# Two transformer layers on one core: column blocks of 512 + 64 in place of 288 + 288 in the MLP output and the projections

## The chip, the cores and the metric

The kernel runs on one core of a Trainium2 chip. The metric is the device time of one execution in microseconds (us), the median of several executions. TensorE, ScalarE, VectorE, GpSimdE and SyncE are called PE, ACT, DVE, POOL and SP, as in the profile. PEld is PE's weight load. L776 is line 776 of the kernel's file; the two files have different line numbers.

## The reference

```python
# B=1, S=2048 tokens, D=576, H=32 heads of 18, window 256, F=4608
def A(x, wqkv, wo):                       # sliding-window causal attention
    q, k, v = split(x @ wqkv)             # (2048 x 576) @ (576 x 1728)
    s = q @ k.T * 18**-0.5                # masked: 0 <= i - j < 256
    return softmax(s) @ v @ wo            # @ (576 x 576)
def Bm(x, w1, b1, w2, b2):
    return gelu(layernorm(x) @ w1 + b1) @ w2 + b2    # 576 -> 4608 -> 576
x = A_x
for _ in range(2):
    x = x + A(layernorm(x), A_wqkv, A_wo)
    x = x + Bm(layernorm(x), B_w1, B_b1, B_w2, B_b2)
```

## The kernel before

The work is cut into 8 chunks: two layers with four chunks of four 128-token tiles each. For every chunk there are projections (`qkv`), attention (`E`, in two halves of four head groups), the attention output (`tail`) and an MLP in two halves of F (`G_part`, `mm2`). Different chunks overlap. While the attention of chunk k runs, PE also does the MLP output of earlier chunks and the projections of the next one. I call this the filling work, because it fills the time in which ACT computes exponentials.

Nothing is ordered at run time. When the kernel is built, its own planner assigns each task a start from assumed costs and emits one fixed order for each engine. It also picks a PSUM bank for each task.

```python
FILL = (6, 5, 4)        # banks for the filling work: projections, attention output, MLP output
MM1 = (0, 1, 2, 3)      # first MLP matmul
SC = (0, 2, 4)          # pairs of banks (0,1), (2,3), (4,5) for the scores; a score group takes two pairs
...
def mm_cost(n):         # assumed time of one matmul of n columns, us
    return max(n / 2400.0, 0.026) + (0.006 if n > 64 else 0.0)
...
def place(t):           # planner: which bank
    ...
    key = (max(bank_free[b] for b in bs), n)     # the bank that has been free longest, then list order
```

Each output row has 576 columns, more than the 512 fp32 columns that the program counts as one PSUM bank (`bank(i)` is `ps[:, i*512:(i+1)*512]`), so every product is cut in columns. Before, the cut is 288 + 288.

```python
def mm2(k, hf, prio):                     # MLP output of one half of F (18 blocks of 128)
    for i in range(nt):                   # four token tiles
        for hh in range(2):               # two halves of 288 columns
            b = Bank(FILL)
            for f0 in range(0, NFH, 6):   # one PE task: 6 matmuls
                ... e.matmul(bank(b)[:, 0:HB], hT[:, fl, tile i], w2_sb[:, fl, hh*HB:(hh+1)*HB],
                             start=(fl == 0), stop=(fl == NFH - 1))
            resid(t, hh, b, prio)         # DVE adds the bank to x: the bank is free after that
def two_out(...):                         # projections and attention output: two banks of 288
    for o in range(2): 5 matmuls of 288 columns (576 = 4.5 x 128 rows, padded with zeros)
# qkv: two_out for q, for k, for v; a DVE cast for each bank
def scores(k, g, parts, prio):            # 32-row matmuls, four at a time; then two exponentials on ACT
    bs = [Bank(SC, True), Bank(SC, True)]
```

The softmax here doesn't subtract the row's maximum and nothing guards it: scores larger than these inputs give would overflow.

## Time and profile before

| what | before |
|---|---|
| median of 6 runs | 985.98 us (983.5 to 988.68) |
| span of the profiled run | 987.9 us |
| PE busy | 949.5 us (96%) |
| next engine: ACT busy | 586.0 us (59%) |

The profiled execution took 989.72 us, a little more than the slowest of the six.

The first lines are from the page of the kernel before: span, busy time with share and number of instructions, and the chain that ended last as shares of the span.

```profile
span 987.9 us, 22924 instructions
PE 949.5 (96%) x9592; PEld 606.9 (61%) x9592; DVE 317.1 (32%) x772; ACT 586.0 (59%) x705; POOL 368.8 (37%) x507
PE 78%; DMA 5%; DVE 5%; POOL 5%; ACT 4%; issue 3%; DVEq 0%; POOLq 0%
```

PE bounds the kernel. The next lines are groups of instructions of the same page: line, engine, operation, tiles, shapes and count, then busy time and the mean of one in ns, then idle time just before them and what ended it.

```profile
L637 ACT ACTIVATE pT<-ps 128x1024 bf16<-128x1024 f32 (+2 forms) x384 | 347.2, 971 | 128.1 <-PE ps L628 126.9
L776 PE MATMUL ps<-w_sb,hT 128*128 128x288 bf16 x2304 | 316.1, 288 | 6.0 <-DVE x_res L709 4.9
L709 DVE TENSOR_TENSOR x_res<-ps,x_res 128x288 f32<-128x288 f32 x160 | 70.7, 449 | 363.4 <-PE ps L776 342.6
L558 PE MATMUL ps<-wqkv,xnTa 128*128 128x288 bf16 x768 | 120.5, 286 | 8.9 <-DVE qn L594 5.0
L509 DVE TENSOR_SCALAR xn<-x_res,mv_all,rstd 128x576 bf16<-128x576 f32 x60 | 47.2, 801 | 26.1 <-POOL rstd L499 14.6
```

The mean of 288 ns is not what a matmul costs in a stream, because the records of successive matmuls overlap. The start times in the trace show that cost. From one L776 matmul to the next the median is 122 ns, from one L751 matmul (512 columns) to the next it is 216 ns, against a mean record of 379 ns.

The first of these lines reads: ACT stood idle for 126.9 us in front of exponentials because it waited for score matmuls (L628).

The waits view says who waited for whom: total us, times, longest.

```profile
PE ps L628 <- ACT pT L637: 8.4, 18, 1.4
PE ps L558 <- DVE qn L594: 5.0, 5, 1.0
PE ps L776 <- DVE x_res L709: 4.9, 10, 0.6
```

### The profile page before, as it was taken

To read this page: it belongs to the slowest core of one execution; us is meant where nothing else is said; L and a number is where in the kernel's file an instruction comes from. 1 tells how busy PE (TensorE), PEld (TensorE's weight loads), DVE (VectorE), ACT (ScalarE), POOL (GpSimd) and SP (SyncE) were. 2 spreads that over 40 slices of the span, in tenths; PEclk is the share of its full clock that TensorE was granted. 3 is DMA by queue.
4 is the path that set the end of the run, shared out by engine and by line. 5 is a ranking of instruction groups with operands and counts; after the bars stand their busy time and mean duration, and the time that the engine had idled before them with its cause. 6 is when DMAs were issued, how large, how long until landed. Compare 5 with 4: busy or idle time off the path is not lost.

```text
span 987.9 us, 22924 instructions
## 1 busy us (share of the span) xinstructions
PE 949.5 (96%) x9592; PEld 606.9 (61%) x9592; DVE 317.1 (32%) x772; ACT 586.0 (59%) x705; POOL 368.8 (37%) x507
## 2 busy tenths in 40 slices
PE   8898889999999999999999999999999999999998
PEld 6665547655575656756476565756567564657556
DVE  5653612722145211534028130361115310132001
ACT  0476676377753777447761777627774487852531
POOL 4555725334333434325153252433333352531000
PEclk9999899999999999999999999999999999999999
DMA  9846380964269250881529542494516816084540
GB/s 195 173 116 136 74 253 15 208 174 138 68 145 192 60 178 28 188 187 34 191 56 204 136 126 80 133 170 106 169 49 167 177 44 198 14 220 118 172 132 25
DMA packets 227287, 129.58 MB, mean 131 GB/s; under 512 B 141808, under 2 KB 225008, under 8 KB 227184
## 3 DMA queue, kind: packets, MB, share of 16 engines
q1 hardware_dynamic: 217872, 120.43, 49.4%
q0 software_dynamic: 6880, 5.03, 2.7%
q10 hardware_dynamic: 2432, 2.65, 0.9%
q8 instruction: 76, 1.25, 0.5%
q14 instruction: 27, 0.22, 0.1%
HBM read 90.69 MB, written 2.36 MB: 94 GB/s over the span
## 4 chain that ended last, share of the span: by engine, by line
PE 78%; DMA 5%; DVE 5%; POOL 5%; ACT 4%; issue 3%; DVEq 0%; POOLq 0%
PE ps L776 29%; PE ps L751 27%; PE ps L558 7%; PE ps L675 7%; PE ps L628 6%; ACT pT L637 3%; POOL pT L658 2%; DMA attT<-attq 2%; DVE x_res L709 2%; PE ps L564 2%; POOL rstd L499 2%; DVE st_all L486 2%; DMA x_res<-in_A_x_dram 1%; DMA kT<-qn 1%; DVE xn L509 1%
## 5 line engine op out<-in xcount | busy, mean ns | idle before, releaser
L637 ACT ACTIVATE pT<-ps 128x1024 bf16<-128x1024 f32 (+2 forms) x384 | 347.2, 971 | 128.1 <-PE ps L628 126.9
L658 POOL TENSOR_SCALAR_AFFINE_SELECT pT<-pT 128x512 bf16<-128x512 bf16 (+1 forms) x368 | 278.1, 778 | 388.2 <-ACT pT L637 365.4
L755 ACT ACTIVATE hT<-ps,b1col 128x512 bf16<-128x512 f32 x288 | 196.5, 687 | 251.1 <-PE ps L751 250.8
L776 PE MATMUL ps<-w_sb,hT 128*128 128x288 bf16 x2304 | 316.1, 288 | 6.0 <-DVE x_res L709 4.9
L751 PE MATMUL ps<-xnTm,w_sb 128*128 128x512 bf16 x1440 | 319.4, 379 | 0.1
L776 PEld LDWEIGHTS ps<-w_sb,hT 128*128 128x128 bf16 x2304 | 211.2, 98 | 80.6 <-issue 20.2
L751 PEld LDWEIGHTS ps<-xnTm,w_sb 128*128 128x128 bf16 x1440 | 139.5, 98 | 159.6 <-issue 0.4
L709 DVE TENSOR_TENSOR x_res<-ps,x_res 128x288 f32<-128x288 f32 x160 | 70.7, 449 | 363.4 <-PE ps L776 342.6
L558 PE MATMUL ps<-wqkv,xnTa 128*128 128x288 bf16 x768 | 120.5, 286 | 8.9 <-DVE qn L594 5.0
L675 PEld LDWEIGHTS ps<-vA,pT 128*128 128x128 bf16 x2880 | 94.2, 96 | 29.2 <-issue 11.7
L675 PE MATMUL ps<-vA,pT 128*128 128x20 bf16 x2880 | 100.6, 172 | 5.6 <-DVE attq L690 2.7
L558 PEld LDWEIGHTS ps<-wqkv,xnTa 128*128 128x128 bf16 x768 | 71.2, 97 | 33.1 <-DVE qn L594 7.8
L628 PE MATMUL ps<-qT,kT 32*128 32x384 bf16 (+2 forms) x1408 | 75.0, 280 | 11.6 <-ACT pT L637 8.4
L594 DVE CAST qn<-ps 128x288 bf16<-128x288 f32 x128 | 57.4, 455 | 39.2 <-PE ps L564 38.3
L486 DVE BATCH_NORM_STATS2 st_all<-x_res 128x6 f32<-128x288 f32 x120 | 50.8, 446 | 17.2 <-DMA x_res<-in_A_x_dram 15.9
L509 DVE TENSOR_SCALAR xn<-x_res,mv_all,rstd 128x576 bf16<-128x576 f32 x60 | 47.2, 801 | 26.1 <-POOL rstd L499 14.6
L564 PE MATMUL ps<-wqkv,xnTa 128*128 128x288 bf16 x192 | 54.9, 286 | 0.0
L628 PEld LDWEIGHTS ps<-qT,kT 32*128 32x128 bf16 x1408 | 22.4, 92 | 49.0 <-issue 24.7
L733 POOL TENSOR_TENSOR x_res<-x_res,b2bc 128x576 f32<-128x576 f32 x32 | 45.2, 1415 | 13.7 <-DVE xn L509 12.9
L712 DVE TENSOR_TENSOR xn<-ps,x_res 128x288 bf16<-128x288 f32 x32 | 14.6, 458 | 110.9 <-PE ps L776 110.9
L497 POOL TENSOR_SCALAR vtmp<-mv_all 128x1 f32<-128x1 f32 (+1 forms) x43 | 8.6, 200 | 103.9 <-DVE mv_all L488 101.4
L685 DVE RECIPROCAL rinv<-ps 128x16 f32<-128x16 f32 x64 | 16.4, 257 | 95.7 <-PE ps L675 95.4
(32 smaller groups left out, 332.7 us busy)
## 6 DMA issues: line engine op xcount, KB each, us to landing
w_sb<-in_B_w_dram SPq DMA_DIRECT2D x144, 288.0 KB, 5.1
w_sb<-in_B_w_dram SPq DMA_DIRECT2D x72, 512.0 KB, 4.0
w_sb<-in_B_w_dram SPq DMA_DIRECT2D x72, 64.0 KB, 3.7
x_res<-in_A_x_dram POOLq DMA_DIRECT2D x4, 1152.0 KB, 7.0
out_dram<-xn SPq DMA_DIRECT2D x16, 144.0 KB, 1.8
wqkv<-in_A_wqkv_dram ACTq DMA_DIRECT2D x3, 576.0 KB, 5.9
hT<-in_A_x_dram SPq DMA_DIRECT2D x1, 576.0 KB, 5.2
wo_sb<-in_A_wo_dram ACTq DMA_DIRECT2D x1, 576.0 KB, 4.0
```

The costliest lines, as they stand in the source:

```text
L486: add("dve", lambda e, i=i, s=s: e.bn_stats(st_all[:, t, i, :], s[:, t, i * HB:(i + 1) * HB]), reads=res, writes=[f"st{t}_{i}"], cost=0.43 ...
L558: ins = e.matmul(bank(bs[o])[:, 0:n], lhs(o, c, full), rhs(o, c, full), start=(c == 0), stop=False)
L564: ins = e.matmul(bank(bs[o])[:, 0:n], lhs(o, 4, full), rhs(o, 4, full), start=False, stop=True)
L594: add("dve", lambda e, o=o, b=bs[o], qv=qv: e.tensor_copy(qv[:, o * 16:(o + 1) * 16, 0:DH], bank(b)[:, 0:HB].rearrange("p (h d) -> p h d", ...
L628: ins = e.matmul(two(bs[j // 2])[:, j % 2, col:col + nq * 128], kT[32 * j:32 * j + 32, g, (T0 + so) % KS, :], qT[32 * j:32 * j + 32, g, qo ...
L637: add("act", lambda e, h2=h2: e.activation(pT[:, sl, 2 * h2:2 * h2 + 2, lo:hi], two(bs[h2])[:, :, lo:hi], ACT.Exp, scale=SCALE), reads=[bs ...
L658: add("pool", lambda e, ap=ap, pat=pat, sgn=sgn, kind=kind: e.affine_select(ap, ap, pattern=pat, compare_op=(ALU.is_ge if kind == "d" else ...
L675: ins = e.matmul(bank(B_O)[:, o:o + VW], pT[:, sl, j, col + qi * 128:col + (qi + 1) * 128], vA[:, (T0 + so) % VS, 4 * g + j, :], start=(fi ...
L709: add("dve", lambda e: e.tensor_tensor(x_res[:, t, sl], bank(b)[:, 0:HB], x_res[:, t, sl], ALU.add), reads=[b], writes=[f"x{t}h{hh}"], cos ...
L751: ins = e.matmul(bank(bk)[:, 0:n], w1_sb[:, sl, col:col + 128], xnTm[:, k % 2, c, 0:n], start=(c == 0), stop=(c == KD - 1))
L755: add("act", lambda e, f=f, fl=fl, bk=bk: e.activation(hT[:, fl, 0:n], bank(bk)[:, 0:n], ACT.Gelu_apprx_tanh, bias=b1col[:, f:f + 1]), rea ...
L776: ins = e.matmul(bank(b)[:, 0:HB], hT[:, fl, i * 128:(i + 1) * 128], w2_sb[:, fl, hh * HB:(hh + 1) * HB], start=(fl == 0), stop=(fl == NFH ...
```

## The change

The cut becomes 512 + 64 (504 + 72 in the projections, where heads of 18 must stay whole). Its intent is to have fewer and longer groups of matmuls, with the short blocks collected in one bank: those of four token tiles in the MLP output, those of q, k and v in the projections. One assumed cost of the planner changes too, from 6 to 4 ns per matmul. The removed `PAIR` branches were dead code.

```diff
-        return max(n / 2400.0, 0.026) + (0.006 if n > 64 else 0.0)
+        return max(n / 2400.0, 0.026) + (0.004 if n > 64 else 0.0)
 # qkv
-            bs = two_out(...)                       # 2 banks x 5 matmuls of 288, for q, k and v each
+        main(0); main(1)                            # 5 matmuls of 504 columns each, a bank each
+        rest((0, 1, 2))                             # 15 matmuls of 72 columns, one bank, start only on the first
+        transpose(0); transpose(1)
+        main(2)
 # tail: 5 x (512 columns, 64 columns) into two banks
 # mm2
-        for i in range(nt):
-            for hh in range(2):                     # 18 matmuls of 288, then resid
+        b = Bank(FILL)
+        for f0 in range(0, NFH, 6):                 # short blocks of four tiles first, one bank
+            for fl in range(f0, f0 + 6):
+                for i in range(nt):
+                    ... e.matmul(bank(b)[:, i*64:(i+1)*64], hT[:, fl, tile i], w2_sb[:, fl, 512:D],
+                                 start=(fl == 0 and i == 0), ...)
+        ... one addition for the four short blocks
+        for i in range(nt):
+            b = Bank(FILL)
+            for f0 in range(0, NFH, 6):             # one PE task: 6 matmuls of 512
+                ... e.matmul(bank(b), hT[:, fl, tile i], w2_sb[:, fl, 0:512], ...)
+            resid(t, 0, b, ...)
 # cuts: resid, ln_stats and pv follow the new columns and heads; PAIR branches removed
```

Four accumulations share one bank here, and only the first matmul carries the start flag. The Trainium skill, "PSUM — Partial Sum Buffer", "The four PSUM rules", names this form as one of two that work: a start clears the written marks of the whole bank, and the other groups' first matmuls find them clear and overwrite.

More of the change, by code (lines that the diff above doesn't have):

```diff
@@ L331, in schedule @@
         return max(t.end for t in self.tasks)
-PAIR = False
-W1W = 2560
 WARM_UNTIL = 140.0
@@ L352, in build_kernel @@
     HB = 288
+    DS = (slice(0, 512), slice(512, 576))
     VW = 20
@@ L373, in build_kernel @@
     x_res = sb("x_res", [P, NT, D], FP32)
-    w1_sb = sb("w1_sb", [P, NB1, W1W], BF16)
+    w1_sb = sb("w1_sb", [P, NB1, 2560], BF16)
     w2_sb = sb("w2_sb", [P, NFH, D], BF16)
@@ L449, in build_kernel @@
     add("pool", lambda e: e.memset(nhalf[:, :], -0.5), writes=["nhalf"], cost=0.1, prio=-10)
-    if not PAIR:
-        add("pool", lambda e: e.memset(xn[:, :, D:KD * 128], 0.0), writes=[f"xn{i}" for i in range(NXN)], cost=0.4, prio=-10)
+    add("pool", lambda e: e.memset(xn[:, :, D:KD * 128], 0.0), writes=[f"xn{i}" for i in range(NXN)], cost=0.4, prio=-10)
     add("pool", lambda e: e.memset(vA[:, :, :, DH:VW], 1.0), writes=[f"v{s}h{h}" for s in range(VS) for h in range(2)], cost=1.6, prio=-8)
@@ L455, in build_kernel @@
             writes=[f"qn{i}h{h}" for h in range(2)], cost=0.5, prio=-9)
-    if not PAIR:
-        add("pool", lambda e: e.memset(attq[:, :, D:KD * 128], 0.0), writes=["aqd"], cost=0.5, prio=-8)
-        add("dve", lambda e: e.memset(wqkv[64:128, 4, :], 0.0), writes=["wqC", "wkC", "wvC"], cost=1.0, prio=-8)
-        add("dve", lambda e: e.memset(wo_sb[64:128, 4, :], 0.0), writes=["woC"], cost=0.4, prio=-8)
-        add("dve", lambda e: e.memset(w1_sb[64:128, :, 2048:2560], 0.0), writes=["w1Z"], cost=1.0, prio=-8)
+    add("pool", lambda e: e.memset(attq[:, :, D:KD * 128], 0.0), writes=["aqd"], cost=0.5, prio=-8)
+    add("dve", lambda e: e.memset(wqkv[64:128, 4, :], 0.0), writes=["wqC", "wkC", "wvC"], cost=1.0, prio=-8)
+    add("dve", lambda e: e.memset(wo_sb[64:128, 4, :], 0.0), writes=["woC"], cost=0.4, prio=-8)
+    add("dve", lambda e: e.memset(w1_sb[64:128, :, 2048:2560], 0.0), writes=["w1Z"], cost=1.0, prio=-8)
     dma("pool", b2bc[:, :], bass.AP(tensor=B_b2.tensor, offset=B_b2.offset, ap=[[0, P], [1, D]]), writes=["b2"], cls="b", ring=2,
@@ L483, in ln_stats @@
         for i in range(2):
-            res = [f"x{t}h{i}"] if srcres is None else [srcres]
+            res = X(t)[:i + 1] if srcres is None else [srcres]
             s = x_res if src is None else src
@@ L512, in ln_norm_T @@
         rd = [f"xn{sl}"]
-        if PAIR:
-            add("dve", lambda e: e.tensor_scalar(xn[:, sl, D:KD * 128], s[:, t, 512:D], mv_all[:, t, 0:1], rstd[:, t:t + 1],
-                                                  op0=ALU.subtract, op1=ALU.mult),
-                reads=res + [f"mv{t}", f"rstd{t}"], writes=[f"xd{sl}"], cost=0.12, prio=prio)
-            rd.append(f"xd{sl}")
         add("sp", lambda e: e.dma_start_transpose(dst[:, :, i * 128:(i + 1) * 128], xn[:, sl, :]),
@@ L533, in w1_load @@
             reads=reads, writes=[f"w1a{sl}"], cls="w1", cost=0.5, prio=prio)
-        if PAIR:
-            src = B_w1[512:576, cols].rearrange("p (a b f) -> p b a f", a=2, b=2)
-            for b in range(2):
-                dma("sp", w1_sb[64 * b:64 * b + 64, sl, 2048:2304].rearrange("p (a f) -> p a f", a=2), src[:, b],
-                    writes=[f"w1b{sl}_{b}"], cls="w1", cost=0.5, prio=prio)
-        else:
-            dma("sp", w1_sb[0:64, sl, 2048:2560], B_w1[512:576, cols], reads=["w1Z"], writes=[f"w1b{sl}_0"], cls="w1", cost=0.5,
-                prio=prio)
+        dma("sp", w1_sb[0:64, sl, 2048:2560], B_w1[512:576, cols], reads=["w1Z"], writes=[f"w1b{sl}_0"], cls="w1", cost=0.5, prio=prio)
     def w2_load(hf, prio, gate=False):
@@ L547, in w2_load @@
                 reads=[f"h{2 * pr}"] if gate else [], writes=[f"w2s{pr}"], cls="w2", ring=9, cost=0.6, prio=prio)
-    def two_out(lhs, rhs, n, reads, prio, after=()):
-        bs = [Bank(FILL), Bank(FILL)]
-        full = slice(0, 128)
-        for o in range(2):
-            def fn(e, o=o):
-                ins = None
-                for c in range(4):
-                    ins = e.matmul(bank(bs[o])[:, 0:n], lhs(o, c, full), rhs(o, c, full), start=(c == 0), stop=False)
-                if PAIR and o == 1:
-                    for oo in range(2):
-                        r = slice(64 * oo, 64 * oo + 64)
-                        ins = e.matmul(bank(bs[oo])[:, 0:n], lhs(oo, 4, r), rhs(oo, 4, r), start=False, stop=True, tile_position=(64 * oo, 0))
-                if not PAIR:
-                    ins = e.matmul(bank(bs[o])[:, 0:n], lhs(o, 4, full), rhs(o, 4, full), start=False, stop=True)
-                return ins
-            w = [bs[0], bs[1]] if (o == 1 and PAIR) else [bs[o]]
-            cost = mm_cost(n) * (4 if PAIR else 5) + (mm_cost(n) * 1.2 if PAIR and o == 1 else 0.0)
-            add("pe", fn, reads=reads, writes=w, cost=cost, prio=prio, alloc=((bs if o == 0 else ()) if PAIR else [bs[o]]), after=after)
-        return bs
     qn_ctr = [0]
-    qn_at = {}
     def qkv(k, i, prio):
@@ L577, in qkv @@
         A = l * NT + t0 + i
-        for n, w in enumerate("qkv"):
-            dest = [f"v{A % VS}h{o}" for o in range(2)] if w == "v" else [f"qn{qn_ctr[0] % NQN}h{o}" for o in range(2)]
-            bs = two_out(lambda o, c, r: xnTa[r, c, i * 128:(i + 1) * 128],
-                         lambda o, c, r, n=n: wqkv[r, c, n * D + o * HB:n * D + (o + 1) * HB], HB,
-                         [f"w{w}A", f"w{w}B", f"w{w}C", f"xa{i}"], prio + 0.01 * n, after=dest)
-            if w == "v":
-                sv = A % VS
-                for o in range(2):
-                    add("dve", lambda e, o=o, b=bs[o]: e.tensor_copy(vA[:, sv, o * 16:(o + 1) * 16, 0:DH],
-                                                                   bank(b)[:, 0:HB].rearrange("p (h d) -> p h d", d=DH)),
-                        reads=[bs[o]], writes=[f"v{sv}h{o}"], cost=0.42, prio=prio)
-            else:
-                sl = qn_ctr[0] % NQN
-                qn_ctr[0] += 1
-                qv = qn[:, sl, :].rearrange("p (h e) -> p h e", e=32)
-                for o in range(2):
-                    add("dve", lambda e, o=o, b=bs[o], qv=qv: e.tensor_copy(qv[:, o * 16:(o + 1) * 16, 0:DH],
-                                                                          bank(b)[:, 0:HB].rearrange("p (h d) -> p h d", d=DH)),
-                        reads=[bs[o]], writes=[f"qn{sl}h{o}"], cost=0.42, prio=prio)
-                if w == "q":
-                    dst, dn = qT[:, :, i * 128:(i + 1) * 128], f"q{i}"
-                else:
-                    dst, dn = kT[:, :, A % KS, :], f"k{A % KS}"
-                add("sp", lambda e, dst=dst, sl=sl: e.dma_start_transpose(dst, qn[:, sl, :]),
-                    reads=[f"qn{sl}h0", f"qn{sl}h1"], writes=[dn], dma="t", ring=8, cost=1.3, lat=2.5, move=0.6, prio=prio)
@@ new lines, in qkv, with main, fn @@
+        sv = A % VS
+        sls = [(qn_ctr[0] + n) % NQN for n in range(2)]
+        qn_ctr[0] += 2
+        views = [qn[:, sl, :].rearrange("p (h e) -> p h e", e=32) for sl in sls] + [vA[:, sv, :, :]]
+        names = [[f"qn{sl}h{o}" for o in range(2)] for sl in sls] + [[f"v{sv}h{o}" for o in range(2)]]
+        wr = lambda n: [f"w{'qkv'[n]}{x}" for x in "ABC"]
+        def main(n):
+            b = Bank(FILL)
+            def fn(e):
+                ins = None
+                for c in range(KD):
+                    ins = e.matmul(bank(b)[:, 0:504], xnTa[:, c, i * 128:(i + 1) * 128], wqkv[:, c, n * D:n * D + 504], start=(c == 0),
+                                   stop=(c == KD - 1))
+                return ins
+            add("pe", fn, reads=wr(n) + [f"xa{i}"], writes=[b], cost=mm_cost(504) * KD, prio=prio + 0.01 * n, alloc=[b], after=names[n][:1])
+            add("dve", lambda e: e.tensor_copy(views[n][:, 0:28, 0:DH], bank(b)[:, 0:504].rearrange("p (h d) -> p h d", d=DH)),
+                reads=[b], writes=names[n][:1], cost=0.68, prio=prio)
@@ new lines, in rest, with fn @@
+        def rest(ns):
+            b = Bank(FILL)
+            def fn(e):
+                ins = None
+                for c in range(KD):
+                    for n in ns:
+                        ins = e.matmul(bank(b)[:, n * 72:(n + 1) * 72], xnTa[:, c, i * 128:(i + 1) * 128],
+                                       wqkv[:, c, n * D + 504:(n + 1) * D], start=(c == 0 and n == ns[0]),
+                                       stop=(c == KD - 1 and n == ns[-1]), skip_group_check=True)
+                return ins
+            add("pe", fn, reads=[r for n in ns for r in wr(n)] + [f"xa{i}"], writes=[b], cost=0.033 * len(ns) * KD, prio=prio, alloc=[b],
+                after=[names[n][1] for n in ns])
+            for n in ns:
+                add("dve", lambda e, n=n: e.tensor_copy(views[n][:, 28:32, 0:DH], bank(b)[:, n * 72:(n + 1) * 72].rearrange("p (h d) -> p h d", d=DH)),
+                    reads=[b], writes=names[n][1:], cost=0.2, prio=prio)
@@ new lines, in transpose @@
+        def transpose(n):
+            if n == 0:
+                dst, dn = qT[:, :, i * 128:(i + 1) * 128], f"q{i}"
+            else:
+                dst, dn = kT[:, :, A % KS, :], f"k{A % KS}"
+            add("sp", lambda e: e.dma_start_transpose(dst, qn[:, sls[n], :]), reads=names[n], writes=[dn], dma="t", ring=8, cost=1.3,
+                lat=2.5, move=0.6, prio=prio)
+        main(0)
+        main(1)
+        rest((0, 1, 2))
+        transpose(0)
+        transpose(1)
+        main(2)
@@ L679, in fn @@
             return ins
-        rd = [f"p{sl}h0", f"p{sl}h1"] + [f"p{sl}m{i}" for i in range(3)] + [f"v{(T0 + p[0]) % VS}h{g // 4}" for p in parts]
+        rd = [f"p{sl}h0", f"p{sl}h1"] + [f"p{sl}m{i}" for i in range(3)] + [f"v{(T0 + p[0]) % VS}h{g // 7}" for p in parts]
         add("pe", fn, reads=rd, writes=[f"pb{B_O}"], cost=0.026 * 4 * sum(p[2] for p in parts), prio=prio, lat=0.2)
@@ L703, in E, with resid @@
             pv(k, *p, prio - 0.1)
-    def resid(t, hh, b, prio, outp=None):
-        src = bank
-        sl = slice(hh * HB, (hh + 1) * HB)
+    def resid(t, hh, b, prio, outp=None, col=0):
+        sl = DS[hh]
+        n = sl.stop - sl.start
         if outp is None:
-            add("dve", lambda e: e.tensor_tensor(x_res[:, t, sl], bank(b)[:, 0:HB], x_res[:, t, sl], ALU.add),
-                reads=[b], writes=[f"x{t}h{hh}"], cost=0.46, prio=prio)
-        else:
-            add("dve", lambda e: e.tensor_tensor(xn[:, outp, sl], bank(b)[:, 0:HB], x_res[:, t, sl], ALU.add),
-                reads=[b, f"x{t}h{hh}"], writes=[f"xn{outp}" if hh == 0 else f"xd{outp}"], cost=0.46, prio=prio)
+            add("dve", lambda e: e.tensor_tensor(x_res[:, t, sl], bank(b)[:, col:col + n], x_res[:, t, sl], ALU.add),
+                reads=[b], writes=[f"x{t}h{hh}"], cost=(0.74, 0.2)[hh], prio=prio)
+        else:
+            add("dve", lambda e: e.tensor_tensor(xn[:, outp, sl], bank(b)[:, col:col + n], x_res[:, t, sl], ALU.add),
+                reads=[b, f"x{t}h{hh}"], writes=[f"xn{outp}"], cost=(0.74, 0.2)[hh], prio=prio)
     def tail(k, prio):
@@ L717, in tail @@
         rd = [f"aq{g}" for g in range(G)]
-        if PAIR:
-            add("dve", lambda e: e.tensor_copy(attq[:, 0:nt, D:KD * 128], attq[:, 0:nt, 512:D]), reads=rd, writes=["aqd"], cost=0.25,
-                prio=prio)
         for i in range(nt):
@@ L725, in tail, with fn @@
             t = t0 + i
-            bs = two_out(lambda o, c, r, i=i: attT[r, c, i * 128:(i + 1) * 128],
-                         lambda o, c, r: wo_sb[r, c, o * HB:(o + 1) * HB], HB, [f"aT{i}", "woA", "woB", "woC"], prio)
+            bs = [Bank(FILL), Bank(FILL)]
+            def fn(e, i=i, bs=bs):
+                ins = None
+                for c in range(KD):
+                    for o in range(2):
+                        ins = e.matmul(bank(bs[o])[:, 0:(512, 64)[o]], attT[:, c, i * 128:(i + 1) * 128], wo_sb[:, c, DS[o]], start=(c == 0),
+                                       stop=(c == KD - 1))
+                return ins
+            add("pe", fn, reads=[f"aT{i}", "woA", "woB", "woC"], writes=bs, cost=KD * (mm_cost(512) + mm_cost(64)), prio=prio, alloc=bs)
             for o in range(2):
@@ L763, in mm2, with fn @@
         l, t0, nt = CH[k]
+        fin = hf == 1 and l == NL - 1
+        osl = [(xn_ctr[0] + i) % NXN for i in range(nt)]
+        if fin:
+            assert nt <= NXN
+            xn_ctr[0] += nt
+        b = Bank(FILL)
+        for f0 in range(0, NFH, 6):
+            def fn(e, b=b, f0=f0):
+                ins = None
+                for fl in range(f0, f0 + 6):
+                    for i in range(nt):
+                        ins = e.matmul(bank(b)[:, i * 64:(i + 1) * 64], hT[:, fl, i * 128:(i + 1) * 128], w2_sb[:, fl, 512:D],
+                                       start=(fl == 0 and i == 0), stop=(fl == NFH - 1 and i == nt - 1), skip_group_check=True)
+                return ins
+            add("pe", fn, reads=[f"h{fl}" for fl in range(f0, f0 + 6)] + [f"w2s{fl // 2}" for fl in range(f0, f0 + 6)], writes=[b],
+                cost=6 * nt * 0.028, prio=prio + 0.05, alloc=((b,) if f0 == 0 else ()))
@@ L764, in mm2 @@
+        if fin:
+            for i in range(nt):
+                resid(t0 + i, 1, b, prio, outp=osl[i], col=i * 64)
+        else:
+            add("dve", lambda e, b=b: e.tensor_tensor(x_res[:, t0:t0 + nt, 512:D], bank(b)[:, 0:nt * 64].rearrange("p (t d) -> p t d", d=64),
+                                                      x_res[:, t0:t0 + nt, 512:D], ALU.add),
+                reads=[b], writes=[f"x{t}h1" for t in range(t0, t0 + nt)], cost=0.4, prio=prio)
         for i in range(nt):
             t = t0 + i
-            fin = hf == 1 and l == NL - 1
@@ L767, in mm2 @@
-            if fin:
-                osl = xn_ctr[0] % NXN
-                xn_ctr[0] += 1
-            for hh in range(2):
-                b = Bank(FILL)
-                for f0 in range(0, NFH, 6):
-                    def fn(e, hh=hh, b=b, f0=f0, i=i):
-                        ins = None
-                        for fl in range(f0, f0 + 6):
-                            ins = e.matmul(bank(b)[:, 0:HB], hT[:, fl, i * 128:(i + 1) * 128], w2_sb[:, fl, hh * HB:(hh + 1) * HB],
-                                           start=(fl == 0), stop=(fl == NFH - 1))
-                        return ins
-                    add("pe", fn, reads=[f"h{fl}" for fl in range(f0, f0 + 6)] + [f"w2s{fl // 2}" for fl in range(f0, f0 + 6)], writes=[b],
-                        cost=6 * mm_cost(HB), prio=prio + 0.05 * i, alloc=((b,) if f0 == 0 else ()))
-                resid(t, hh, b, prio, outp=(osl if fin else None))
@@ L782, in mm2, with fn @@
-            if fin:
-                dma("sp", out_dram[t * P:(t + 1) * P, :], xn[:, osl, 0:D], reads=[f"xn{osl}", f"xd{osl}"], cls="o", ring=4, cost=0.5,
+            b = Bank(FILL)
+            for f0 in range(0, NFH, 6):
+                def fn(e, b=b, f0=f0, i=i):
+                    ins = None
+                    for fl in range(f0, f0 + 6):
+                        ins = e.matmul(bank(b), hT[:, fl, i * 128:(i + 1) * 128], w2_sb[:, fl, 0:512], start=(fl == 0), stop=(fl == NFH - 1))
+                    return ins
+                add("pe", fn, reads=[f"h{fl}" for fl in range(f0, f0 + 6)] + [f"w2s{fl // 2}" for fl in range(f0, f0 + 6)], writes=[b],
+                    cost=6 * mm_cost(512), prio=prio + 0.05 * i, alloc=((b,) if f0 == 0 else ()))
@@ L784, in mm2 @@
+            resid(t, 0, b, prio, outp=(osl[i] if fin else None))
+            if fin:
+                dma("sp", out_dram[t * P:(t + 1) * P, :], xn[:, osl[i], 0:D], reads=[f"xn{osl[i]}"], cls="o", ring=4, cost=0.5,
                     prio=prio)
```

## The prediction

> **What bounds the kernel.** TensorE. In the page's first part PE is busy 949.5 of 987.9 us (96%). The next engine is ACT with 586.0. The chain that ended last is 78% PE. The waits view gives PE's waits only a few us per cause: L628 for ACT 8.4, L558 for DVE 5.0, L776 for DVE 4.9. From start to start of successive matmuls in the trace, the median is 215.8 ns at 512 columns (L751), 122.4 ns at 288 (L776, L558, L564) and 25 ns at 20 (L675). So a matmul costs columns/2.4 GHz plus about 2.3 ns, and the weight load in front of each hides even under 20 columns. The Trainium skill ("TensorE: Matmul & The Clock Gate", "Back-to-back issue gap" and "Wait — 56ns, not 53.3ns?") gives the same form, N/2.4 + 2.5 ns, with a floor near 25 ns. The trace agrees with both.
>
> **What the change removes, adds and moves.** It removes 2304 + 960 + 320 = 3584 matmuls of 288 columns and adds as many: 1792 of 504 or 512 columns and 1792 of 64 or 72. Columns and count are unchanged, so with a linear cost nothing is gained:
> - 288 twice: 2 x 122.4 = 244.8 ns.
> - 512 + 64: 215.8 + 29.0 (estimate from the line through the two measured points) = 244.8 ns.
> - The total is 439 us both ways.
>
> The unknown is the short matmul. At the floor (26 ns) the kernel gains about 5 us; at 33 ns it loses about 7.
>
> DVE work stays about the same. A 288-column read of PSUM takes 449 to 455 ns. I estimate 0.70 us for 512 and 0.22 for 64 or 72.
>
> **What lies on the critical path.** What can be gained are PE's stalls when a PSUM bank changes hands. After 140 us the start times show stalls that recur in each step: about 0.72 us between two L776 groups, 0.45 us before a score group, 0.8 to 1.2 us inside the projections. That is some 19 us. The change has 80 bank groups in the MLP output instead of 128, and 4 per projection tile instead of 6, so fewer handovers. Each lasts longer (0.7 us read instead of 0.45), and a long fill can hold a bank that the scores want. I expect 3 to 7 us gained. In the first 140 us, 280 warming matmuls (39.5 us busy) fill time that latency sets; the new order (q and k before the joint short block, v last) moves that by a microsecond or two, either way.
>
> **Predicted time:** 982 us, 80% range 969 to 994. Chances: faster by over 2% 0.05, within 2% 0.91, slower by over 2% 0.04.
>
> **What in the profile shows each step right or wrong.**
> - Start to start within the short group: 29 ns (25 to 31). Long: 216 and 212.5.
> - Matmuls in all 9592 plus or minus the warming ones; PE busy time itself is no guide, since a record includes the pipeline's drain, so short ones look dear.
> - In the waits view, L776's successor waits for the residual addition less in total than 6 us; the projections' wait for casts is less than 6.7.
> - DVE busy falls by 3 to 12 us. ACT and POOL stay within 1%.
>
> **What would make it wrong.** Short matmuls paced by their weight loads when 24 follow each other or when long and short alternate, at 35 ns or more: over 10 us slower. A static order, planned with new costs, that starves ACT of score banks: PE's wait for ACT far above 8.4 us.

## The result, and the profile after

| | before | after |
|---|---|---|
| median | 985.98 us | 989.69 us |
| range of 6 runs | 983.5 to 988.68 | 987.84 to 991.89 |
| ratio, 95% interval | | 1.0037 (1.0016 to 1.0058) |

A ratio is the mean time of one kernel's fast runs over that of the other's of the same rounds, so it is not quite the ratio of the medians quoted. The profile is of the slowest of the six, so that the two traces differ by 2.2 us and the medians by 3.7. The time lies inside the predicted range, but on the other side of zero: 3.7 us slower where 4 us faster was expected.

From the page of the changed kernel, the same parts:

```profile
span 990.1 us, 22748 instructions
PE 942.0 (95%) x9473; PEld 493.5 (50%) x9587; DVE 301.8 (30%) x736; ACT 587.4 (59%) x705; POOL 370.5 (37%) x507
PE 82%; POOL 4%; issue 4%; DMA 4%; DVE 3%; ACT 2%; SPq 1%; POOLq 0%; DVEq 0%
```

```profile
L625 ACT ACTIVATE pT<-ps 128x1024 bf16<-128x1024 f32 (+2 forms) x384 | 348.0, 972 | 175.2 <-PE ps L616 174.9
L787 PE MATMUL ps<-w_sb,hT 128*128 128x512 bf16 x1089 | 259.7, 379 | 9.1 <-issue 4.0
L768 PE MATMUL ps<-w_sb,hT 128*128 128x64 bf16 x1152 | 39.4, 195 | 4.6 <-DVE x_res L697 4.6
L697 DVE TENSOR_TENSOR x_res<-ps,x_res 128x512 f32<-128x512 f32 x112 | 60.2, 549 | 302.3 <-PE ps L787 245.7
L553 PE MATMUL ps<-wqkv,xnTa 128*128 128x504 bf16 x480 | 115.4, 379 | 3.5 <-DMA xnTa<-xn 1.7
L506 DVE TENSOR_SCALAR xn<-x_res,mv_all,rstd 128x576 bf16<-128x576 f32 x60 | 41.2, 694 | 39.9 <-DMA xnTm<-xn 22.0
```

Its waits view, the lines that answer to those before:

```profile
PE ps L616 <- ACT pT L625: 9.9, 13, 1.4
PE ps L768 <- DVE x_res L697: 4.6, 10, 0.5
PE ps L787 <- DVE x_res L697: 2.0, 4, 0.5
PE ps L567 <- DVE qn L557: 1.0, 2, 0.5
```

The projections' wait for casts fell from 6.7 us (5.0, and 1.7 for v) to 2.3 (the 1.0 shown, and 0.7 and 0.6 for v). ACT's idle time in front of the exponentials has grown from 126.9 to 174.9 us. PE's wait for ACT in the waits view hardly moved (8.4 to 9.9).

PE's busy time fell by 7.5 us while the kernel became slower. Only 9473 matmuls have a record, of 9587 weight loads, and the records overlap. I therefore worked from the start times of matmuls. Each matmul gets its cost in an undisturbed stream, 122.4 ns for 288 columns, 215.8 for 512, 212.5 for 504, 29.0 for 64, 32.4 for 72 and so on. Entering or leaving the 32-row score matmuls is counted apart, up to 100 ns each time. What remains is called a stall. Missing records were filled in from the program's order.

| us, from start times of PE | before | after |
|---|---|---|
| work: sum of stream costs | 865.4 | 865.0 |
| entering and leaving the score matmuls | 33.8 | 29.9 |
| warming matmuls at the start, with their gaps | 48.4 | 47.5 |
| stalls before 140 us | 6.3 | 7.8 |
| stalls from 140 to 800 us | 27.3 | 22.6 |
| stalls after 800 us | 2.1 | 12.4 |

The work is the same. In the middle, the change gains 4.7 us of stalls; after 800 us it loses 10.3. The fall in the line of the score matmuls is mostly an artefact of the filling in: a missing record that is put at the end of its run of matmuls hides the step to the score group behind it, and the time is counted as a stall. A recount that places the missing records by their start times gives 34.9 and 33.5 us for that line, 29.0 and 20.4 us for the middle, and 2.3 and 12.1 us after 800 us. So stalls are to be read to within about 2 us, and the gain in the middle is 5 to 9 us. The loss is in the last chunk's attention. The next two fences give busy us (and instructions) by stretch in the order PE, PEld, DVE, ACT, POOL, then the granted clock, DMA share and GB/s; first before, then after. Both stretches are the end of the first half of that attention.

```profile
805.00:810.00 5.00, 5.00 (x78) 3.78 (x76) 1.18 (x4) 2.67 (x3) 2.45 (x5) 1.00 0.10 33
810.00:815.00 5.00, 5.00 (x83) 3.58 (x76) 0.92 (x2) 4.38 (x5) 3.04 (x4) 1.00 0.09 31
815.00:820.00 5.00, 4.59 (x70) 3.05 (x68) 1.17 (x3) 4.25 (x6) 3.32 (x5) 1.00 0.59 162
```

```profile
805.00:810.00 5.00, 4.42 (x68) 2.36 (x60) 1.25 (x3) 3.35 (x5) 3.39 (x4) 1.00 0.92 292
810.00:815.00 5.00, 2.43 (x56) 1.34 (x50) 0.72 (x2) 5.00 (x7) 3.65 (x5) 0.59 0.87 273
815.00:820.00 5.00, 4.98 (x39) 2.35 (x39) 0.00 (x0) 3.71 (x6) 2.19 (x4) 0.73 0.00 0
```

From 810 to 815 us the roles are swapped: ACT is busy all the time, PE for 2.43 us of 5, and the granted clock drops. How it came to this is in the timeline of ACT in the changed kernel just before (start, us busy, what, and the idle time before it):

```profile
796.22 1.94 ACT L625 ACTIVATE pT<-ps 128x1024 bf16<-128x1024 f32 x2 [1.49 <-PE ps L616]
799.64 1.94 ACT L625 ACTIVATE pT<-ps 128x1024 bf16<-128x1024 f32 x2 [1.49 <-PE ps L616]
803.07 1.94 ACT L625 ACTIVATE pT<-ps 128x1024 bf16<-128x1024 f32 x2 [1.49 <-PE ps L616]
805.19 1.94 ACT L625 ACTIVATE pT<-ps 128x1024 bf16<-128x1024 f32 x2 [0.18 <-PE ps L616]
808.60 7.44 ACT L625 ACTIVATE pT<-ps 128x1024 bf16<-128x1024 f32 x8 [1.48 <-PE ps L616]
```

Two exponentials take 1.94 us, and then ACT waits 1.49 us for the next scores, because PE is busy with filling work. At 808 us the filling work is used up while the exponentials of four score groups are still to come (the last piece, 7.44 us), and PE can only go at their pace. From the same window of PE, the lines of score groups and the last filling work (other lines left out):

```profile
805.07 2.76 PE L787 MATMUL ps<-w_sb,hT 128*128 128x512 bf16 x12
809.68 0.40 PE L616 MATMUL ps<-qT,kT 32*128 32x384 bf16 x8
811.51 0.61 PE L616 MATMUL ps<-qT,kT 32*128 32x384 bf16 x8 [1.44 <-ACT pT L625]
813.34 0.61 PE L616 MATMUL ps<-qT,kT 32*128 32x256 bf16 x8 [0.69 <-ACT pT L625]
```

In the kernel before, ACT has the scores early in the same stage and works on, 5.80 us in one piece:

```profile
799.93 5.80 ACT L637 ACTIVATE pT<-ps 128x1024 bf16<-128x1024 f32 x6 [0.37 <-PE ps L628]
807.22 1.94 ACT L637 ACTIVATE pT<-ps 128x1024 bf16<-128x1024 f32 x2 [1.49 <-PE ps L628]
```

In the last chunk's attention alone, ACT's wait for scores rose by 6.0 us. From the waits views of 780 to 890 us, first before, then after:

```profile
ACT pT L637 <- PE ps L628: 9.2, 12, 1.5
ACT pT L625 <- PE ps L616: 15.2, 14, 1.5
```

In earlier chunks the projections of the next chunk are further filling work for the second half. After the last chunk there is no later attention that could absorb a delay.

### The profile page after: what moved, and what is told of

Same layout as the page of the kernel before. It is cut to its first block, busy times and chain, and to the rows that moved or that the text cites. A ratio compares the mean times of both kernels' runs of the same rounds, so it can differ in the third digit from the quotient of the medians.

```text
span 990.1 us, 22748 instructions
## 1 busy us (share of the span) xinstructions
PE 942.0 (95%) x9473; PEld 493.5 (50%) x9587; DVE 301.8 (30%) x736; ACT 587.4 (59%) x705; POOL 370.5 (37%) x507
## 4 chain that ended last, share of the span: by engine, by line
PE 82%; POOL 4%; issue 4%; DMA 4%; DVE 3%; ACT 2%; SPq 1%; POOLq 0%; DVEq 0%
PE ps L744 29%; PE ps L787 24%; PE ps L553 9%; PE ps L663 6%; PE ps L616 4%; PE ps L717 4%; PE ps L768 4%; POOL pT L646 3%; ACT pT L625 2%; PE ps L567 2%; DVE x_res L697 1%; PE ps L472 1%; DMA attT<-attq 1%; DMA x_res<-in_A_x_dram 1%; DMA qT<-qn 1%
## 5 line engine op out<-in xcount | busy, mean ns | idle before, releaser
L625 ACT ACTIVATE pT<-ps 128x1024 bf16<-128x1024 f32 (+2 forms) x384 | 348.0, 972 | 175.2 <-PE ps L616 174.9
L744 PE MATMUL ps<-xnTm,w_sb 128*128 128x512 bf16 x1395 | 319.5, 382 | 2.8 <-issue 0.5
L787 PE MATMUL ps<-w_sb,hT 128*128 128x512 bf16 x1089 | 259.7, 379 | 9.1 <-issue 4.0
L744 PEld LDWEIGHTS ps<-xnTm,w_sb 128*128 128x128 bf16 x1440 | 137.8, 98 | 162.3 <-issue 4.6
L787 PEld LDWEIGHTS ps<-w_sb,hT 128*128 128x128 bf16 x1152 | 102.3, 98 | 125.7 <-issue 16.0
L697 DVE TENSOR_TENSOR x_res<-ps,x_res 128x512 f32<-128x512 f32 x112 | 60.2, 549 | 302.3 <-PE ps L787 245.7
L553 PE MATMUL ps<-wqkv,xnTa 128*128 128x504 bf16 x480 | 115.4, 379 | 3.5 <-DMA xnTa<-xn 1.7
L553 PEld LDWEIGHTS ps<-wqkv,xnTa 128*128 128x128 bf16 x480 | 42.2, 98 | 50.8 <-issue 4.5
L557 DVE CAST qn<-ps 128x504 bf16<-128x504 f32 x64 | 43.6, 681 | 41.5 <-PE ps L553 41.2
L506 DVE TENSOR_SCALAR xn<-x_res,mv_all,rstd 128x576 bf16<-128x576 f32 x60 | 41.2, 694 | 39.9 <-DMA xnTm<-xn 22.0
L717 PE MATMUL ps<-wo_sb,attT 128*128 128x512 bf16 (+1 forms) x314 | 43.5, 284 | 2.2 <-DMA attT<-attq 1.0
L768 PE MATMUL ps<-w_sb,hT 128*128 128x64 bf16 x1152 | 39.4, 195 | 4.6 <-DVE x_res L697 4.6
```

What stands on the lines that cost most here:

```text
L553: ins = e.matmul(bank(b)[:, 0:504], xnTa[:, c, i * 128:(i + 1) * 128], wqkv[:, c, n * D:n * D + 504], start=(c == 0), stop=(c == KD - 1))
L625: add("act", lambda e, h2=h2: e.activation(pT[:, sl, 2 * h2:2 * h2 + 2, lo:hi], two(bs[h2])[:, :, lo:hi], ACT.Exp, scale=SCALE), reads=[bs ...
L697: add("dve", lambda e: e.tensor_tensor(x_res[:, t, sl], bank(b)[:, col:col + n], x_res[:, t, sl], ALU.add), reads=[b], writes=[f"x{t}h{hh} ...
L717: ins = e.matmul(bank(bs[o])[:, 0:(512, 64)[o]], attT[:, c, i * 128:(i + 1) * 128], wo_sb[:, c, DS[o]], start=(c == 0), stop=(c == KD - 1))
L744: ins = e.matmul(bank(bk)[:, 0:n], w1_sb[:, sl, col:col + 128], xnTm[:, k % 2, c, 0:n], start=(c == 0), stop=(c == KD - 1))
L768: ins = e.matmul(bank(b)[:, i * 64:(i + 1) * 64], hT[:, fl, i * 128:(i + 1) * 128], w2_sb[:, fl, 512:D], start=(fl == 0 and i == 0), stop= ...
```

## The experiments

Four theories were tested.
- A: the longer PE tasks of filling work (6 x 216 ns = 1.3 us instead of 6 x 122 = 0.73 us) make scores wait, so ACT is fed late.
- B: a 512-column group holds its PSUM bank for longer (18 x 216 ns = 3.9 us of PE time instead of 2.2, plus the read). Where that is bank 4 or 5, the third pair of score banks is missing. A score group takes two pairs, so with three pairs the next scores can start after the first exponential, with two pairs only after the second.
- C: the time follows from the luck of the planner's order.
- P: the projections' split gains time in itself.

Results first, so that the single experiments can be read against them. "ACT's wait" is the total that ACT waited for score matmuls, by the waits view. The last column comes from the order made at build time, not from the chip: how many of the last chunk's 24 score groups use the third pair of banks, (4,5). The stalls come from one trace of each kernel. The last chunk's attention begins some 10 to 30 us before 800 us, so its stalls can exceed those after 800 us. Each ratio rests on six runs of the kernel, but on five for e4 and four for e10.

| kernel | ratio to before (95%) | ACT's wait, us | stalls 140 to 800 us | stalls in the last chunk's attention | third pair, of 24 |
|---|---|---|---|---|---|
| before | 1 | 126.9 | 27.3 | 2.8 | 14 |
| after | 1.0037 (1.0016 to 1.0058) | 174.9 | 22.6 | 12.4 | 12 |
| e1, after, blocks of 3 | 1.0000 (0.9980 to 1.0019) | 139.4 | 20.0 | 11.0 | 10 |
| e2, before, blocks of 9 | 1.0039 (1.0021 to 1.0057) | 143.4 | 29.5 | 4.7 | 14 |
| e3, MLP output alone | 1.0073 (1.0055 to 1.0091) | 181.6 | 26.2 | 12.3 | 12 |
| e4, projections alone | 0.9925 (0.9911 to 0.9940) | 120.9 | 17.4 | 2.8 | 14 |
| e5, before, 4 ns constant | 0.9944 (0.9928 to 0.9960) | 123.3 | 18.4 | 2.8 | 14 |
| e6, projections alone, 6 ns | 0.9928 (0.9912 to 0.9945) | 122.9 | 19.0 | 2.8 | 14 |
| e7, before, banks held twice as long | 1.0058 (1.0041 to 1.0075) | 167.2 | 23.8 | 12.2 | 10 |
| e8, e1 with the 512 blocks on bank 6 | 0.9978 (0.9958 to 0.9997) | 110.4 | 18.7 | 3.8 | 16 |
| e9, after, rule of banks | 0.9945 (0.9929 to 0.9961) | 150.0 | 13.1 | 11.2 | 10 |
| e10, e1, rule of banks | 0.9903 (0.9888 to 0.9918) | 140.0 | 10.8 | 9.1 | 8 |
| e11, e4, rule for filling work | 0.9948 (0.9930 to 0.9965) | 99.8 | 22.5 | 1.6 | 14 |
| e12, e5, rule of banks | 0.9946 (0.9927 to 0.9964) | 127.1 | 20.7 | 6.0 | 10 |

All twelve are correct against the reference.

### e1: shorter PE tasks in the changed kernel

```diff
-            for f0 in range(0, NFH, 6):      # 6 matmuls of 512 in one task
+            for f0 in range(0, NFH, 3):      # 3
```

> The changed kernel, with the 512-column MLP output planned in blocks of 3 matmuls (0.65 us) instead of 6 (1.3 us). Same matmuls. Theory A (the long fill blocks delay the score matmuls, ACT starves, and in the last chunk the filling work runs out before the attention does): ACT's idle time ahead of the exponentials falls from 175 us to about the 128 us of before, the stalls after 800 us shrink from about 13 to about 3 us, time 978 to 984. Theory B (a fill that holds bank 4 or 5 for 3.9 us keeps score bank pairs away): nothing changes, 988 to 991. Theory C (the static order is a lottery): anything within 980 to 995 with no change in the idle time of ACT.

Measured: 988.7 us against 988.06 for before in the same rounds. ACT's wait fell to 139.4 us, three quarters of the way back. The stalls of the last chunk's attention did not: 12.4 to 11.0 us. The time is the one that B expected, the waits of ACT are those of A. So A explains the long waits of ACT, but not the loss at the end. The timeline of ACT shows what is left, a regular 0.83 us:

```profile
797.79 1.94 ACT L625 ACTIVATE pT<-ps 128x1024 bf16<-128x1024 f32 x2 [0.83 <-PE ps L616]
800.55 1.94 ACT L625 ACTIVATE pT<-ps 128x1024 bf16<-128x1024 f32 x2 [0.83 <-PE ps L616]
803.33 1.94 ACT L625 ACTIVATE pT<-ps 128x1024 bf16<-128x1024 f32 x2 [0.84 <-PE ps L616]
```

Each pair of exponentials is followed by a gap of one size. That is what one score group in flight looks like: the next scores start only when both exponentials have ended.

### e2: longer PE tasks in the kernel before

```diff
-                for f0 in range(0, NFH, 6):  # 6 matmuls of 288 in one task
+                for f0 in range(0, NFH, 9):  # 9
```

> The kernel before, with its 288-column MLP output planned in blocks of 9 matmuls (1.1 us) instead of 6 (0.73 us). Theory A: ACT's idle time ahead of the exponentials rises from 128 us by 20 us or more, and the time by 3 to 10 us. Theory B: no change, since a bank is held for 2.2 us as before. Theory C: within 5 us either way.

Measured: 991.44 us, ratio 1.0039. ACT's wait rose by 16.5 us (expected 20 or more), and the time by about 3.4 us. Longer tasks came with a few us more, but the new order that they bring may do as much (a new order alone moves e5 by 0.56%), so the time is not shown to be theirs. The end of the kernel is touched only a little (4.7 us of stalls).

### e3 and e4: the two parts of the change alone

e3 takes `mm2` of the change with `qkv` and `tail` of before; e4 takes `qkv` and `tail` of the change with `mm2` of before. Both have the 4 ns constant.

> Only the MLP output is split 512 + 64; the projections are as before. Theory A and B: the loss in the last chunk is all here, so stalls after 800 us stay at 10 us or more; time 986 to 993. The gain before 800 us (about 4 us of stalls) is partly lost, since the projections wait for casts as before.

> Only the projections are split; the MLP output is as before. Theory A and B: no loss in the last chunk (stalls after 800 us about 3 us), and the projections' waits for casts (6.7 us before) mostly gone: 978 to 984, faster than both kernels.

Measured: e3 995.05 us, a little beyond what was expected, and e4 980.71 us. So the small result of the whole change hides two opposite effects of about 7 us each, which do not quite add up to it: the kernel with the MLP output's split loses, and the one with the projections' split gains. The loss at the end is in e3 (12.3 us of stalls) and not in e4 (2.8).

### e5 and e6: is e4's gain due to the split, or to the constant?

```diff
 # e5: the kernel before with
-        return max(n / 2400.0, 0.026) + (0.006 if n > 64 else 0.0)
+        return max(n / 2400.0, 0.026) + (0.004 if n > 64 else 0.0)
 # e6: e4 with the reverse
```

> The kernel before with one planning constant of the change alone: 4 ns instead of 6 ns of assumed overhead per matmul. Same matmuls, another static order. Theory P (splitting the projections removes their waits for casts and bank handovers, which is what made the projections-only kernel 7 us faster): this one stays at 984 to 989. Theory C (that gain came from the planner's constant or from the luck of the order): 980 to 983, with the projections' stalls down.

> The projections-only kernel planned with the old constant of 6 ns. Theory P: still 979 to 984. Theory C: back to 985 to 990.

Measured: e5 982.4 us, e6 980.65 us. Theory P missed on e5, and theory C missed on e6. Each of the two edits alone removes nearly the same stalls in the middle (27.3 to 18.4 and 19.0 us), and both together (e4, 17.4) remove hardly more. The lines for the projections' waits on DVE in e5:

```profile
PE ps L558 <- DVE vA L586: 1.8, 1, 1.8
PE ps L558 <- DVE qn L594: 0.3, 1, 0.3
```

Before, the second of these was 5.0 us. So the wait that the split of the projections removes is one that the old order had put there, and one number in the planner removes it as well.

With that, the right base for the parts is the kernel before with the change's constant, e5. Against it the projections' split is worth about nothing (0.9925 to 0.9944), and the MLP output's split costs 1.3% (1.0073 to 0.9944), or 1.1% where the projections are split too (1.0037 to 0.9925): 11 to 13 us, estimates worked out from ratios of two sets of rounds. By the table this cost is not at the end alone: the last chunk's stalls are about 9.5 us higher (12.3 and 2.8, 12.4 and 2.8), and those in the middle are 8 and 5 us higher (26.2 and 18.4, 22.6 and 17.4), or 7 and 4 by the recount.

### e7: the bank hold by itself

The kernel before, with its two 288-column halves taken in turn, block by block. The matmuls and the length of a task stay the same; two banks are held together, each about twice as long.

```diff
-            for hh in range(2):
-                b = Bank(FILL)
-                for f0 in range(0, NFH, 6):
+            bs = [Bank(FILL), Bank(FILL)]
+            for f0 in range(0, NFH, 6):
+                for hh in range(2):
```

> The kernel before, where the two 288-column halves of an MLP output tile take turns block by block, so that two PSUM banks are held together for twice as long; same matmuls, same blocks of 6. Theory B (a fill that holds bank 4 or 5 for longer keeps a pair of score banks away, so only one score unit is in flight and ACT waits before each pair of exponentials): ACT's idle time ahead of the exponentials rises from 127 us by 15 us or more, and the time by 4 to 12 us. Theory A (only the length of a block matters): within 2 us of before.

Measured: 992.96 us, ratio 1.0058. This line of its waits view stands against 126.9 us before:

```profile
ACT pT L637 <- PE ps L628: 167.2, 122, 27.5
```

Stalls in the last chunk's attention rose from 2.8 to 12.2 us. This reproduces the loss of the change at the end without a matmul of 512 columns and without longer tasks. A cannot do that. Two limits belong to it. The dose is larger than the change's: by the plan, MLP outputs hold banks 4 and 5 for 163 us before, 194 us after the change and 295 us in e7. And 0.58% of time is no more than the 0.56% that the planner's constant moved in e5, so the time alone could be the order's. The stalls in the last chunk's attention could hardly be: they stay at 2.8 us in e4, e5 and e6, whose orders differ from the one before by the constant, the projections or both.

### e8: the hold taken off the score banks

```diff
-            b = Bank(FILL)       # 512-column MLP output of e1
+            b = Bank((6,))
```

> The changed kernel with blocks of 3, and the 512-column MLP output kept to bank 6 alone, so that it never takes a score bank. Theory B: the regular 0.83 us gaps before pairs of exponentials (56 between 140 and 775 us in the kernel with blocks of 3) go, ACT's idle time at the exponentials falls from 139 to 115 or less, and the last chunk's stalls after 800 us fall from 11 us to 5 or less; the price is a wait of about 0.9 us at each of the 64 handovers of bank 6 that no other PE work covers, so the time may still be 985 to 1000. Theory A: no change of the gaps.

Measured: 985.84 us, ratio 0.9978. ACT's wait for scores fell from 139.4 us in e1 to this:

```profile
ACT pT L625 <- PE ps L616: 110.4, 105, 30.2
```

Gaps of 0.7 to 0.95 us between 140 and 775 us fell from 56 to 22, so they did not all go. In the last chunk's attention 3.8 us of stalls are left. The expectation for the stalls after 800 us (5 us or less) failed as it was written, since there were 11.7. They sit elsewhere: after 889 us, where no attention is left to cover a handover, PE waits 0.95 us six times and 1.70 us twice for the one bank. B holds for the attention, and the price that was expected is visible.

### e9 to e12: another rule for choosing banks

The planner took the bank that had been free longest, and so handed banks 4 and 5 to filling work while bank 6 was free. The new rule takes the first bank of the list among those free by the time the task starts.

```diff
-                    key = (max(bank_free[b] for b in bs), n)
+                    key = (max(max(bank_free[b] for b in bs), now), n)
 # e9: in the changed kernel; e10: in e1; e12: in e5 (288 + 288, 4 ns)
 # e11: in e4, for the filling work alone
```

> The changed kernel with one rule of its planner altered: among PSUM banks that are free by the time a matmul group starts, it takes the first in the group's list (6, then 5, then 4 for the filling work; 0 and 2 before 4 for the scores) instead of the one that has been free longest. By the plan, MLP outputs then hold banks 4 and 5 for 94 us in place of 194. Theory B (held score banks starve ACT): ACT's idle time at the exponentials falls from 175 us to 145 or less, the last chunk's stalls after 800 us from 12 us to 6 or less, time 975 to 984. If the long hold is not the cause: ACT's idle time stays within 10 us of 175 and the time within 987 to 992.

> The same rule of banks in the kernel with blocks of 3. Theory A and B both hold in part: this removes both causes, so ACT's idle time at the exponentials is 110 to 130 us, stalls after 800 us at most 4 us, and the time 972 to 981, as fast as the projections-only kernel or faster. If it stays above 985, something else in the MLP output's split costs the time.

> The projections-only kernel with the rule of banks for the filling work alone (6 where it is free, then 5, then 4). A try for the fastest: 974 to 981 if score banks are still held too long there, 981 or more if not.

> The old 288 + 288 split with the planner's constant of 4 ns and the rule of banks for all groups, as in the fastest kernel so far (the changed kernel with blocks of 3 and that rule, 977.1 us); its blocks of 6 x 122 ns are 0.73 us long, those of the fastest 0.65. If the column split is worth nothing in itself, because columns and matmuls are the same, and only the planning differs, this one lands within 3 us of it: 974 to 980. If fewer and longer bank groups are worth something once the banks are chosen well, it is slower: 981 or more. If the shorter hold of the score banks is worth more, it is faster: below 974.

Measured: e9 981.47, e10 977.06, e11 981.98 and e12 981.46 us, beside 986.98, 986.98, 986.98 and 986.22 us for the kernel before. e9 has the expected time, but not by the expected way. ACT's wait fell only to 150.0 us (145 or less was expected), and the last chunk's stalls stayed. The gain is in the middle, where stalls fell from 22.6 to 13.1 us. The rule also applies to the scores, and by the plan it leaves them the third pair in only 10 of the last 24 groups. So e9 is no clean test of B. e10 missed its two detailed expectations in the same way, and is nevertheless the fastest kernel: 0.97% under the kernel before, below e4's 0.75%.

```profile
span 974.5 us, 22760 instructions
PE 932.3 (96%) x9472; PEld 490.4 (50%) x9592; DVE 300.0 (31%) x736; ACT 589.0 (60%) x705; POOL 372.0 (38%) x507
```

e11 came out on the "if not" side of its expectation. It has the smallest wait of ACT (99.8 us) and the smallest stalls at the end (1.6 us), yet is not faster than e4: its stalls in the middle rose from 17.4 to 22.5 us. Its waits view names a new wait, of the attention output on its transposed input:

```profile
PE ps L717 <- DMA attT<-attq: 5.8, 4, 2.0
```

e12 is the old split under the same rule and nearly the same length of task as e10. Its median is just inside "slower" of what was expected (981 or more). e10 is faster than e12, with intervals that do not touch. But 0.4% is less than the 0.56% that one planning constant moved in e5, so these runs don't show that the 512 + 64 split is better in itself.

## Why the prediction was right or wrong

**The cost of the matmuls: right.** "With a linear cost nothing is gained" was the main step. Short matmuls started 29 ns apart (32 for 72 columns), long ones 216 and 212 ns; the sum of work is 865.4 us before and 865.0 after. The weight loads did not pace the short ones, neither in rows nor in alternation with long ones (28 ns).

**DVE: right in direction, too small.** Busy time fell by 15.3 us, where 3 to 12 were predicted. Of this, 6.0 us are in the layer norm's subtraction and scaling (L509, L506), which the change leaves alone: 47.2 to 41.2 us. Without them the fall is 9.3 us, inside the range. In the traces this instruction mostly takes 486 to 659 ns (median 579 before, 578 after), but 751 to 1654 ns in 21 of 60 cases before and in 10 of 60 after. In 30 of these 31 slow cases a selection or addition of POOL was running when it started, and it ended 0.31 to 0.32 us after POOL's instruction did. The Trainium skill, "Perfetto Trace Analysis", "Optimizing Scalar/DVE Operations", says that GpSimdE and VectorE share an SBUF read port, and this trace agrees.

**Stalls that the handovers of banks cause: right for the middle.** "I expect 3 to 7 us gained" was said of them, and from 140 to 800 us the change gained 4.7 (5 to 9 by the recount). But the reason given, fewer handovers, is not the whole one. In the projections, the stall was made by the static order, and e5 removes most of it with no change of columns. For the MLP output the predicted sign was wrong in the waits view: PE's waits for the additions are 7.5 us together (L768 4.6, L787 2.0, and 0.9 more of L787 for the joint addition of the short blocks), where "less in total than 6 us" was predicted and 6.0 were measured before (4.9, and 1.1 for the last additions).

**The step that failed: the price of a longer hold.** The prediction wrote that "a long fill can hold a bank that the scores want" and put no number to it. With the constant held equal, the MLP output's split loses an estimated 11 to 13 us (e3 to e5, after to e4). Holding two banks for twice as long, with nothing else of the change, brings the same stalls in the last chunk's attention (e7, 12.2 us; its time rose by 5.7 us, 0.58% of the kernel before), and keeping the long blocks off the score banks takes most of them away (e8, 11.0 to 3.8 us). That accounts for the loss at the end. The 4 to 8 us that the split costs in the middle are not in e7 (23.8 us, below before's 27.3), and their cause stays open. Over all 14 kernels, those whose plan gives the third pair to at least 14 of the last 24 score groups have at most 4.7 us of such stalls, and those with 12 or fewer have at least 6.0. The last column of the table is a plan and not a measurement, so this is a strong hint rather than a proof; e7 and e8 are the experiments. That the measured time still lies in the predicted range is in part luck: the loss at the end and the gain in the middle, neither put on the right scale, nearly cancel.

**The sign to watch was the wrong one.** "PE's wait for ACT far above 8.4 us" did not come; it was 9.9. What moved was ACT's wait for PE, 126.9 to 174.9 us. Idle time of an engine with 59% load looked free. In the last chunk it was not, since ACT's work in the attention is a fixed amount, and delaying it moves it to where PE has nothing left to fill with. The total of that wait is no guide: e10 is the fastest kernel with 140.0 us, and e11 has the least, 99.8.

**The clock, of which nothing was predicted.** Its mean was 0.991 before and 0.986 after in the profiled executions, and 0.990 or 0.991 in the other five of the changed kernel. In the changed kernel the clock was at half speed for 6.8 us from 810.9 us and again from 865.5 us, both times after PE had starved. At half speed that is at most 3.4 us of PE's time each time. The 512-column matmuls (L744) in these two stretches started about 427 ns apart instead of 216, which adds up to 3.3 us, so about a quarter of the 12.4 us is this echo. The traces of all 14 kernels split in the same way: the clock falls to half between 800 and 900 us in the seven kernels with 12 or fewer groups on the third pair, and in none of the seven with 14 or more.

**What stays open.** The orders of all these kernels differ in many places at once. One assumed cost moved the time by 0.56%. How much of e9's, e10's and e12's differences is the rule and how much is the order's luck can't be told from these runs.

## What to carry to other kernels

First find whether an edit changes the cost of the work at all: here two cuts with equal columns and equal numbers of matmuls cost the same to within 0.4 us in 865, so only waits could change. When a group of matmuls grows, count how long it holds its PSUM bank and who else wants that bank; if it is the engine that feeds a slower partner, test the hold by itself, as e7 does, before blaming the size of the matmuls. In a statically ordered kernel, plan the kernel before with the change's constants too, since otherwise a gain that belongs to a constant is put down to the change.

## What the Trainium skill lacked or had wrong

- "TensorE: Matmul & The Clock Gate", "Back-to-back issue gap", gives about 131 ns per matmul as the sustained rate at 512 columns with a weight load each, and calls columns/2.4 + 2.5 ns an overestimate there (another section of the page, "Wait — 56ns, not 53.3ns?", has measured 215.7). Here matmuls of 512 columns with a weight load each started 215.8 ns apart over whole stages, and 122.4 ns at 288 columns: the formula holds, the 131 ns do not.
- The same page and section puts everything from 1 to 64 columns at the floor of about 25 ns. Here 20 columns took 25 to 26 ns, but 64 columns 28 to 29 ns and 72 columns 32 ns: 64 is already on the line.
- The same page, "HAM oscillation — how this bites in real kernels", ties the drop to half clock to PE-idle gaps over about 3.4 us. Its next section, "A second HAM failure mode: psum-queue depth-cycling", has frequent short pauses do it too, but says neither how long nor how many. Here the clock fell to half at 810.9 us, when the longest idle gap of PE nearby was 1.44 us (it spans the drop); in about 3.41 us before it PE had been busy for 2.11 us. So no single long gap is needed.
- "TensorEngine Tiling (Array Packing)", "Key Properties", says that a change of tiling mode drains TensorE, but gives no time for it. Here a score group (32-row tiles) started 218 ns after a 288-column matmul that otherwise takes 122, and a full-array matmul 263 ns after a 384-column score group that otherwise takes 163: about 100 ns each way, 33.8 us in the kernel before (entered from a 20-column matmul it is less, 103 ns instead of 25).
- "Perfetto Trace Analysis" does not warn that matmul records can be missing unevenly between two traces: none of 9592 before, 114 of 9587 after, which lowers PE's busy time by itself.
